# Pinning the early transfers of queries, keys, values and weight chunks to program order

## The chip, the cores and the metric

The kernel runs on one core of one Trainium2 chip. The metric is device time in microseconds (us), the median over several runs. An execution covers the whole chain: attention, a two-layer MLP, and a top-1 mixture of experts.

## The reference

Only what matters for the computation is kept:

```python
# attention: q, k, v are (4, 12, 448, 64)
scores = np.matmul(q, k.transpose(0, 1, 3, 2)) / np.sqrt(64)
scores = np.where(np.triu(np.ones((448, 448), bool), k=1), -1e9, scores)
attn = np.exp(scores - scores.max(-1, keepdims=True))
x = np.matmul(attn / (attn.sum(-1, keepdims=True) + 1e-9), v)   # -> (1792, 768)
# first MLP: w_in (768, 2048), w_out (2048, 768)
h = x @ w_in
x = (h - np.tanh(h)) @ w_out
# second: 8 experts, one for each token by argmax(x @ w_gate)
#   out = gate * sigmoid(x @ w_output_gate) * (relu(x @ w1[e]) @ w2[e])
```

All of it is float32. The kernel reaches that precision in the wide matmuls by splitting an operand into a high and a low part and adding three products.

## The kernel before

Attention works on 24 pairs of heads, six for each of four batch entries. For a pair, TensorE makes the scores of two heads (L351 for the first six pairs, in which the two heads sit in the two halves of the array's rows; L342 from the seventh pair on, with split operands), VectorE adds the mask and takes the row maxima (L371), ScalarE takes the exponential (L379), TensorE transposes the probabilities (L409), ScalarE or VectorE copy them out of PSUM (L417, L419, L423), and TensorE multiplies them with the values (L448). For the first six pairs the row sums are spread by small matmuls (`pd`, L432), VectorE multiplies the value with their reciprocals (L453, tile `ds`), ScalarE makes the high part (L461, `xh`) and VectorE the low part (L463, `xl`) of the result, which is the input of the first MLP.

The weights `w_in` come as sixteen raw chunks of 768 KB each (L142). A `Decoder` turns each into floats: one multiplication on ScalarE (L149), three operations on VectorE (L155, L156, L159), and then the split on ScalarE and VectorE (L84, L85). One or two are decoded for each pair, as the list `DECODE` says; each time the second step ends, the next chunk is fetched. `w_out` follows in the same way and goes back to memory.

The main loop runs over pairs and, within one, over a list of steps (`EARLY` for the first six, `ORDER` for the others): S scores, P transposes of the pair before, F the last score rows of the pair after, N the sums, A the value of the pair before. Loads of pair n + 2 are written at step N of pair n. From the first pair of the second batch on, matmuls of the first MLP (L480) are filled in between the steps; in the first batch only two groups of them run ahead, six matmuls a pair. Short dummy matmuls (L509, `warm`) stand between the steps of the first two pairs, pinned to program order.

All these instructions go through a scheduler that orders each engine's queue itself, by what it takes to be ready; each engine then works through its queue strictly in that order, and a waiting instruction holds up all behind it. `keep_in_program_order` pins an instruction behind the one that was written before it for the same engine. SyncE issues nearly all transfers, so its queue is the order of the transfers. Buffers matter too: `v` has two buffers, so the values of pair n + 2 wait for the value matmuls of pair n; `qh` and `kh` have two each, and from the seventh pair on `q` and `k` one each.

Of the kernel before, what the change touches and what calls it, by code (L numbers as in the profile page):

```python
# [19 lines left out]
P = 128  # L20
# [26 lines left out]
SCORES2 = 6  # L47

AHEAD = 2

LATER = (1, 1, 2, 2, 1, 0, 0, 0)

# [3 lines left out]
class Weights:  # L56


    def __init__(self, nc, pool, nslots):
        self.nc = nc  # L60
        self.slots = [(pool, n) for n in range(nslots)]
        self.pos = 0
# [60 lines left out]
class Decoder:  # L123
# [4 lines left out]
    def __init__(self, nc, stage):  # L128
        self.nc, self.stage = nc, stage
        self.jobs, self.ready, self.done, self.state = [], [], [], None  # L130


    keep = staticmethod(lambda x: x)

    def add(self, src, place, then):

# [2 lines left out]
    def fetch(self, n=1):  # L139
        for src, place, then in self.jobs[:n]:  # L140
            raw = place()
            self.nc.sync.dma_start(raw.rearrange("p a b -> p (a b)"), src)  # L142
            self.ready.append((raw, then))
        del self.jobs[:n]

# [7 lines left out]
    def second(self):  # L153
        vec, y, raw = self.nc.vector, self.y, self.raw
        self.keep(vec.tensor_scalar(y, y, 3, None, op0=ALU.logical_shift_left))  # L155
        vec.scalar_tensor_tensor(  # L156
            y, raw[:, :, 0], 29, y, op0=ALU.logical_shift_right, op1=ALU.bitwise_or
        )
        vec.scalar_tensor_tensor(  # L159
            y, raw[:, :, 1], -(1 << 31), y, op0=ALU.bitwise_and, op1=ALU.bitwise_or  # L160
        )
        self.done.append((y.bitcast(F32), self.ready.pop(0)[1]))
        self.fetch()

    def third(self):
        y, then = self.done.pop(0)
# [38 lines left out]
def attention_mlp1(tc, consts, ring, qk, v, w_in, w_out, wo, gT):  # L205


    nc = tc.nc
# [7 lines left out]
    NB = S // P  # L216
    TL = S - NB * P
# [10 lines left out]
    QC = 2 * S + TL  # L228
# [25 lines left out]
    stage = ctx.enter_context(tc.tile_pool(name="stage", bufs=1))  # L254
    dec = Decoder(nc, stage)
    win = []
    dec.keep = tc.keep_in_program_order
    free = [n for n in range(NF // 2, NF)] + [n for n in range(3 * NF // 4, NF)] + [NF - 2, NF - 1]

    def aside():  # L260
# [13 lines left out]
    def flush():  # L274
        while late:
            late.pop(0)()

    class Pair:
        def __init__(self, n):
            self.n, self.b, self.hp = n, n // NP, n % NP  # L280
            self.pr = prs[n % 2]
            self.two = n >= SCORES2

            self.divided = n >= NP

        def load(self):
            if self.two:
                self.q = ap.tile([P, QC], F32, tag="q", name="q", bufs=1)
                self.k = ap.tile([P, 2 * S], F32, tag="k", name="k", bufs=1)
            else:  # L290
                self.q = ap.tile([P, QC], F32R, tag="qh", name="q").bitcast(F32)
                self.k = ap.tile([P, 2 * S], F32R, tag="kh", name="k").bitcast(F32)
            for h in range(2):
                eng = nc.scalar if self.n == 0 and h else nc.sync
                s = slice(h * D, (h + 1) * D)

                c = slice(0, QC) if self.two else slice(h * (S + TL), h * (S + TL) + S)
                eng.dma_start(self.q[s, c], qk[self.n][:, c])
                c = slice(0, 2 * S) if self.two else slice(h * S, (h + 1) * S)
                eng.dma_start(self.k[s, c], qk[self.n][:, QC + c.start:QC + c.stop])  # L300

        def load_v(self):
            vt = ap.tile([P, NK, 2 * D], F32, tag="v", name="v")
            nc.sync.dma_start(
                vt[:, :NB], v[self.n, :NB * P].rearrange("(p c) d -> p c d", c=NB)
            )
            nc.sync.dma_start(vt[:TL, NB], v[self.n, NB * P:])
            self.v = vt.rearrange("p c (j d) -> p c j d", j=2)

        def split(self):  # L310
# [158 lines left out]
    def ahead(kd):  # L469

        for f in range(2):
            if kd == 0:
                begun.append(mps.tile([P, S], F32, tag="h", name="h"))
            for _ in mlp1_part(0, xT[0], f, begun[f], kd):
                pass
# [9 lines left out]
    def mlp1(b, xT, after=None):  # L485
        for f in range(NF):
            has = b == 0 and f < len(begun)
            ph = begun[f] if has else mps.tile([P, S], F32, tag="h", name="h")
            for kd in range(KD - 1 if has else 0, KD):
                for n in mlp1_part(b, xT, f, ph, kd):  # L490
                    if kd == KD - 1 and n == 2:
                        g = mp.tile([P, S], F32, tag="g", name="g", bufs=2)
                        nc.scalar.activation(g, ph, AF.Tanh)  # L493
                        nc.vector.tensor_tensor(g, ph, g, op=ALU.subtract)  # L494
                        nc.sync.dma_start(gT[f * P:(f + 1) * P, b * S:(b + 1) * S], g)
                        if after:
                            after(f)
                    yield
# [7 lines left out]
    def keep_busy(n):  # L506
        for _ in range(n):
            ph = mps.tile([P, S], F32, tag="h", name="warm")
            x = nc.tensor.matmul(  # L509
                ph.rearrange("p (a b) -> p a b", a=2), idle[:, :P],  # L510
                idle.unsqueeze(1).to_broadcast([P, 2, S // 2]), start=True, stop=True,
            )
            tc.keep_in_program_order(x)
# [10 lines left out]
    for i in range(len(pairs) + 1):  # L524
        cur = pairs[i] if i < len(pairs) else None
        nxt = pairs[i + 1] if i + 1 < len(pairs) else None
        prv = pairs[i - 1] if i > 0 else None
        todo = DECODE[i] if i < len(DECODE) else 0
        order = EARLY if i < NP else ORDER
        total = sum(FILL.get(o[0], 0) for o in order)  # L530
        begin = [n * len(order) // todo for n in range(todo)]
        acc, done = 0.0, 0
        for step, (op, *arg) in enumerate(order):
            if op == "F" and i + 1 < NP:
                nxt.score((rows[-1],))
            elif op == "S" and cur:
                cur.score(*arg)
            elif op == "N" and cur:
                cur.norm(*arg)
                if i + 2 < len(pairs):  # L540
                    pairs[i + 2].load()
                    pairs[i + 2].load_v()
                if i == 0:
                    dec.fetch(3)
            elif op == "P" and prv:
                prv.turn_p(*arg)
            elif op == "A" and prv:
                prv.value(xT[prv.b])
            elif op == "T" and nxt:
                nxt.split()  # L550
            if i < 2:
                keep_busy(WARM[i + 1])
            if 2 <= i <= NP and step == AHEAD:
                ahead(i - 2)
            acc += FILL.get(op, 0) * (per_b0 if i <= 2 * NP else per) / total
            fill.run(round(acc) - done)
            done = round(acc)
            flush()
            if i == 3:
                dec.keep = lambda x: x  # L560
            if dec.tick(bool(begin) and step >= begin[0]):
                begin.pop(0)
        if prv and prv.hp == NP - 1 and prv.b < B - 1:
            fill.add(mlp1(prv.b, xT[prv.b]))
# [649 lines left out]
def fused(ctx, tc, qk, v, w_in, w_out, gw, gates, w12, out):  # L1214
# [42 lines left out]

    consts["turnover"] = turnover
    last = attention_mlp1(tc, consts, ring, qk, v, w_in, w_out, wo, gT)

    xg, early, late, close = mlp2_route(
# [66 lines left out]
```

## Time and profile before

| what | value |
|---|---|
| median of 3 runs | 1017.88 us (1017.08 to 1018.27) |
| profiled execution, own time | 1015.92 us |
| its span, first to last instruction | 1014.2 us |
| TensorE matmuls busy | 989.7 us (98%) |
| TensorE weight loads busy | 894.6 us (88%) |
| VectorE busy | 651.1 us (64%) |
| ScalarE busy | 485.8 us (48%) |
| moved by DMA | 176.50 MB, mean 174 GB/s |

The shares are means over stages with different limits. Of the profile's page, the line of 40 slices shows where: the weight loads are at four to eight tenths in the first five slices and at eight or nine tenths nearly everywhere behind them, while VectorE is at seven to nine tenths in slices two to seven. A slice is 25 us. So the change, which touches the first 150 us or so, has to be read from that stretch alone.

### The profile page before, as it was taken

How to read it: one execution, taken by the hardware profiler on the slowest of the kernel's cores; microseconds unless marked ns; L12 is line 12 of the kernel's file. 1: busy time of each engine (PE TensorE's matmuls, PEld its weight loads, DVE VectorE, ACT ScalarE, POOL GpSimd, SP SyncE). 2: the span in 40 equal slices, each digit the busy share in tenths (PEclk: the TensorE clock that was granted, in tenths of full speed). 3: DMA queues.
4: the chain of work that ended last, by engine and by line, in shares of the span. 5: the costliest groups of instructions: out<-in, count | busy, mean ns of one | idle time of the engine just before them, and what ended most of it. 6: DMA issues, size and time to landing. Idle time of an engine off the chain costs nothing.

```text
span 1014.2 us, 16674 instructions
## 1 busy us (share of the span) xinstructions
PE 989.7 (98%) x6166; PEld 894.6 (88%) x6166; DVE 651.1 (64%) x1453; ACT 485.8 (48%) x1021; POOL 77.3 (8%) x84
## 2 busy tenths in 40 slices
PE   9999999999999999999999999999899999999995
PEld 4566788888888889999999999989899999999995
DVE  5779898877877635436776777375664754665430
ACT  5678888676766534312121212263643654555330
POOL 1000000000000000000111112102211011111000
PEclk9999999999999999999999999999999999999998
DMA  8844556767665228462434252497767765774400
GB/s 287 204 126 131 164 177 195 238 195 220 210 208 185 105 97 262 145 206 77 145 90 144 59 146 90 120 338 220 254 220 237 240 213 155 253 250 131 182 9 33
DMA packets 89100, 176.50 MB, mean 174 GB/s; under 512 B 8818, under 2 KB 52072, under 8 KB 89010
## 3 DMA queue, kind: packets, MB, share of 16 engines
q1 hardware_dynamic: 84258, 157.37, 49.4%
q0 software_dynamic: 4304, 16.97, 5.1%
q8 instruction: 50, 0.82, 0.3%
q10 hardware_dynamic: 448, 1.02, 0.3%
q14 instruction: 40, 0.33, 0.1%
HBM read 142.81 MB, written 34.08 MB: 174 GB/s over the span
## 4 chain that ended last, share of the span: by engine, by line
PE 83%; DMA 6%; DVE 5%; ACT 3%; issue 2%; SPq 0%; POOL 0%; POOLq 0%; ACTq 0%; DVEq 0%
PE x2p L688 22%; PE h L480 18%; PE h L1103 14%; PE py L1123 14%; PE x L448 4%; PE pt L409 3%; PE s L342 3%; DMA k<-in_qk_dram 2%; PE s L351 2%; DMA glo<-gT 2%; PE tr L1091 1%; DMA wraw<-in_w_dram 1%; DMA wo<-dy 1%; DVE w L85 1%; PE warm L509 1%
## 5 line engine op out<-in xcount | busy, mean ns | idle before, releaser
L480 PE MATMUL h<-xh,w 128*128 128x448 f32 x768 | 228.1, 375 | 1.3 <-ACT xh L461 0.7
L688 PE MATMUL x2p<-w,ghi 128*128 128x384 f32 x896 | 228.9, 336 | 0.0
L688 PEld LDWEIGHTS x2p<-w,ghi 128*128 128x128 f32 x896 | 160.9, 188 | 0.3 <-issue 0.2
L1103 PE MATMUL h<-xh,w 128*128 128x256 f32 x864 | 156.9, 284 | 4.2 <-DVE h L1110 2.6
L1123 PE MATMUL py<-w,h 128*128 128x384 f32 x864 | 155.2, 336 | 0.0
L688 PE MATMUL x2p<-w,glo 128*128 128x384 f32 x448 | 149.9, 335 | 0.0
L1123 PEld LDWEIGHTS py<-w,h 128*128 128x128 f32 x864 | 149.1, 188 | 0.0
L480 PEld LDWEIGHTS h<-xh,w 128*128 128x128 f32 x768 | 138.3, 189 | 11.8 <-ACT xh L461 1.8
L85 DVE TENSOR_TENSOR w<-wraw,w 128x768 fp32r<-128x768 f32 x144 | 131.8, 954 | 21.3 <-ACT w L84 21.3
L480 PE MATMUL h<-xl,w 128*128 128x448 f32 x384 | 142.9, 374 | 0.0
L1103 PEld LDWEIGHTS h<-xh,w 128*128 128x128 f32 x864 | 134.7, 191 | 5.2 <-DVE h L1110 2.8
L84 ACT CAST w<-wraw 128x768 fp32r<-128x768 f32 x144 | 114.0, 830 | 36.8 <-PE py L1123 28.5
L1103 PE MATMUL h<-xl,w 128*128 128x256 f32 x432 | 122.1, 283 | 0.0
L379 ACT ACTIVATE pr<-pr,mx 128x384 f32<-128x384 f32 (+3 forms) x168 | 88.3, 527 | 54.5 <-DVE mx L371 48.2
L711 DVE CUSTOM_DVE_ANT_0 junk<-x,row 128x768 bf16<-128x768 f32 x88 | 84.2, 957 | 32.9 <-ACT x L697 30.6
L688 PEld LDWEIGHTS x2p<-w,glo 128*128 128x128 f32 x448 | 84.1, 188 | 0.2 <-issue 0.2
L1103 PEld LDWEIGHTS h<-xl,w 128*128 128x128 f32 x432 | 82.6, 191 | 0.4 <-issue 0.4
L480 PEld LDWEIGHTS h<-xl,w 128*128 128x128 f32 x384 | 72.1, 188 | 5.3 <-DVE dy L155 0.3
L371 DVE CUSTOM_DVE_ANT_0 pr<-s,mask 128x384 f32<-128x384 f32 (+1 forms) x144 | 57.0, 419 | 13.8 <-PE s L342 10.4
L494 DVE TENSOR_TENSOR g<-h,g 128x448 f32<-128x448 f32 x64 | 39.8, 622 | 38.5 <-ACT g L493 38.1
L409 PE MATMUL pt<-ident,pr 128*128 128x128 f32 x384 | 61.0, 275 | 2.7 <-ACT pT L417 1.3
L409 PEld LDWEIGHTS pt<-ident,pr 128*128 128x128 f32 x384 | 46.7, 140 | 16.9 <-DVE pT L419 2.5
(178 smaller groups left out, 1159.0 us busy)
## 6 DMA issues: line engine op xcount, KB each, us to landing
wraw<-in_w_dram SPq DMA_DIRECT2D x144, 384.0 KB, 5.4
gT<-g SPq DMA_DIRECT2D x64, 224.0 KB, 1.9
glo<-gT SPq DMA_DIRECT2D x14, 1024.0 KB, 7.0
draw<-in_w_out_dram SPq DMA_DIRECT2D x16, 768.0 KB, 4.6
raw<-in_w_in_dram SPq DMA_DIRECT2D x14, 768.0 KB, 8.6
q<-in_qk_dram SPq DMA_DIRECT2D x36, 240.0 KB, 4.1
k<-in_qk_dram SPq DMA_DIRECT2D x36, 224.0 KB, 4.3
wo<-dy SPq DMA_DIRECT2D x16, 384.0 KB, 3.4
```

The source lines that it names most:

```text
L84: self.nc.scalar.copy(t[:, 0, :], raw)
L85: self.nc.vector.tensor_tensor(t[:, 1, :], raw, t[:, 0, :].bitcast(F32), op=ALU.subtract)
L371: nc.vector.tensor_tensor_reduce(out=self.probs(r), in0=s[:, o[n]:o[n] + w], in1=m, scale=-0.125, scalar=3.0e38, op0=ALU.add, op1=ALU.min, ...
L379: nc.scalar.activation(pc, pc, AF.Exp, bias=self.mx[:, x:x + 1], scale=-1.0, accum_out=self.sm[:, x:x + 1],)
L409: nc.tensor.transpose(pt[:, n * P:(n + 1) * P], self.pr[:, o:o + P], ident)
L448: nc.tensor.matmul(px[j * D:(j + 1) * D, kc * P:], self.v[:n, kc, j, :], self.pT[:n, j, pcol[kc]:pcol[kc] + S - kc * P], start=(kc == 0), ...
L480: nc.tensor.matmul(ph, w[:, kd, :], x, start=(kd == 0 and n == 0), stop=(kd == KD - 1 and n == 2))
L494: nc.vector.tensor_tensor(g, ph, g, op=ALU.subtract)
L688: nc.tensor.matmul(px, a[:, f, :], w[:, 0, h * hn:(h + 1) * hn], start=(n == 0), stop=(n == 3 * NF - 1),)
L711: nc.vector.tensor_tensor_reduce(out=junk, in0=x2, in1=row, scale=1.0, scalar=0.0, op0=ALU.mult, op1=ALU.add, accum_out=to,)
L1103: nc.tensor.matmul(ph, wp[:, kd, :], a[:, kd].rearrange("p a b -> p (a b)"), start=(n == 0), stop=(n == 3 * KD - 1),)
L1123: nc.tensor.matmul(py, hs[f][a][:, c], w[:, 0, o * hn:(o + 1) * hn], start=(n == 0), stop=(n == 3 * KF - 1),)
```

## The change

The transfers of the raw chunks (L142) and of the first ten pairs' queries, keys and values (L298, L300, L304, L307) are pinned to program order on SyncE. The chunks are pinned until the loop is at the ninth pair. The chunks fetched at the start are still two, but at the end of the first pair four are asked for instead of three, and until then a decoded chunk asks for no new one (`hold`).

```diff
--- before.py
+++ after.py
@@ -48,6 +48,8 @@
 
 AHEAD = 2
 
+ORDERED = 10
+
 LATER = (1, 1, 2, 2, 1, 0, 0, 0)
 
 WARM = (12, 3, 1)
@@ -128,9 +130,10 @@
     def __init__(self, nc, stage):
         self.nc, self.stage = nc, stage
         self.jobs, self.ready, self.done, self.state = [], [], [], None
-
-
-    keep = staticmethod(lambda x: x)
+        self.hold = True
+
+
+    keep = ask = staticmethod(lambda x: x)
 
     def add(self, src, place, then):
 
@@ -139,7 +142,7 @@
     def fetch(self, n=1):
         for src, place, then in self.jobs[:n]:
             raw = place()
-            self.nc.sync.dma_start(raw.rearrange("p a b -> p (a b)"), src)
+            self.ask(self.nc.sync.dma_start(raw.rearrange("p a b -> p (a b)"), src))
             self.ready.append((raw, then))
         del self.jobs[:n]
 
@@ -160,7 +163,8 @@
             y, raw[:, :, 1], -(1 << 31), y, op0=ALU.bitwise_and, op1=ALU.bitwise_or
         )
         self.done.append((y.bitcast(F32), self.ready.pop(0)[1]))
-        self.fetch()
+        if not self.hold:
+            self.fetch()
 
     def third(self):
         y, then = self.done.pop(0)
@@ -254,7 +258,7 @@
     stage = ctx.enter_context(tc.tile_pool(name="stage", bufs=1))
     dec = Decoder(nc, stage)
     win = []
-    dec.keep = tc.keep_in_program_order
+    dec.keep = dec.ask = tc.keep_in_program_order
     free = [n for n in range(NF // 2, NF)] + [n for n in range(3 * NF // 4, NF)] + [NF - 2, NF - 1]
 
     def aside():
@@ -280,6 +284,8 @@
             self.n, self.b, self.hp = n, n // NP, n % NP
             self.pr = prs[n % 2]
             self.two = n >= SCORES2
+
+            self.ask = tc.keep_in_program_order if n < ORDERED else lambda x: x
 
             self.divided = n >= NP
 
@@ -295,16 +301,16 @@
                 s = slice(h * D, (h + 1) * D)
 
                 c = slice(0, QC) if self.two else slice(h * (S + TL), h * (S + TL) + S)
-                eng.dma_start(self.q[s, c], qk[self.n][:, c])
+                self.ask(eng.dma_start(self.q[s, c], qk[self.n][:, c]))
                 c = slice(0, 2 * S) if self.two else slice(h * S, (h + 1) * S)
-                eng.dma_start(self.k[s, c], qk[self.n][:, QC + c.start:QC + c.stop])
+                self.ask(eng.dma_start(self.k[s, c], qk[self.n][:, QC + c.start:QC + c.stop]))
 
         def load_v(self):
             vt = ap.tile([P, NK, 2 * D], F32, tag="v", name="v")
-            nc.sync.dma_start(
+            self.ask(nc.sync.dma_start(
                 vt[:, :NB], v[self.n, :NB * P].rearrange("(p c) d -> p c d", c=NB)
-            )
-            nc.sync.dma_start(vt[:TL, NB], v[self.n, NB * P:])
+            ))
+            self.ask(nc.sync.dma_start(vt[:TL, NB], v[self.n, NB * P:]))
             self.v = vt.rearrange("p c (j d) -> p c j d", j=2)
 
         def split(self):
@@ -541,7 +547,8 @@
                     pairs[i + 2].load()
                     pairs[i + 2].load_v()
                 if i == 0:
-                    dec.fetch(3)
+                    dec.fetch(4)
+                    dec.hold = False
             elif op == "P" and prv:
                 prv.turn_p(*arg)
             elif op == "A" and prv:
@@ -556,6 +563,8 @@
             fill.run(round(acc) - done)
             done = round(acc)
             flush()
+            if i == ORDERED - 2:
+                dec.ask = lambda x: x
             if i == 3:
                 dec.keep = lambda x: x
             if dec.tick(bool(begin) and step >= begin[0]):
```

Tile names carry numbers below where rows would read alike; the line numbers of the changed kernel are six higher for most lines (L351 is L357, L371 is L377, L448 is L454, L453 is L459, L463 is L469) and three higher in the decoder.

On SyncE, before, behind the second pair's loads (`raw` are chunks; `q_275` and `k_276` belong to the third pair, `q_389` to the fourth):

```order
L142 DMA raw9_161<-in_w_in_dram 128x1536
L142 DMA raw10_201<-in_w_in_dram 128x1536
L142 DMA raw11_249<-in_w_in_dram 128x1536
L142 DMA raw12_284<-in_w_in_dram 128x1536
L298 DMA q_275<-in_qk_dram 64x448
L300 DMA k_276<-in_qk_dram 64x448
L298 DMA q_275<-in_qk_dram 64x448
L300 DMA k_276<-in_qk_dram 64x448
L142 DMA raw13_286<-in_w_in_dram 128x1536
L142 DMA raw14_288<-in_w_in_dram 128x1536
L142 DMA raw15_333<-in_w_in_dram 128x1536
L298 DMA q_389<-in_qk_dram 64x448
```

and in the changed kernel (`q_271`, `k_272` and `v_277` belong to the third pair, `q_387` to the fourth):

```order
L304 DMA q_271<-in_qk_dram 64x448
L306 DMA k_272<-in_qk_dram 64x448
L304 DMA q_271<-in_qk_dram 64x448
L306 DMA k_272<-in_qk_dram 64x448
L310 DMA v_277<-in_v_dram 128x384
L313 DMA v_277<-in_v_dram 64x128
L145 DMA raw10_280<-in_w_in_dram 128x1536
L145 DMA raw11_282<-in_w_in_dram 128x1536
L145 DMA raw12_284<-in_w_in_dram 128x1536
L145 DMA raw13_286<-in_w_in_dram 128x1536
L145 DMA raw14_331<-in_w_in_dram 128x1536
L304 DMA q_387<-in_qk_dram 64x448
```

The third pair's queries, keys and now also its values stand in front of five chunks, and the fourth pair's queries and keys behind these.

On TensorE, before, around the second pair's value (`x_524`; `s_497`, `s_538` and `s_539` are scores of the fourth pair):

```order
L351 MATMUL s_497<-k_390,q_389 64x448 x2
L448 MATMUL x_524<-pT_443,v_158 64x448
L409 MATMUL pt_491<-ident_64,pr1_111 128x128 x2
L448 MATMUL x_524<-pT_443,v_158 64x448
L351 MATMUL s_538<-k_390,q_389 128x384
L432 MATMUL pd_513<-ident_64,sm_261 64x128 x6
L432 MATMUL pd_513<-ident_64,sm_261 64x64 x2
L448 MATMUL x_524<-pT_443,v_158 64x320 x2
L448 MATMUL x_524<-pT_443,v_158 64x192 x2
L448 MATMUL x_524<-pT_443,v_158 64x64 x2
L351 MATMUL s_539<-k_390,q_389 128x384
L351 MATMUL s_538<-k_390,q_389 128x128
```

and in the changed kernel, around the third pair's value (`x_631`), where the fourth pair's first scores (`s_495`) now stand:

```order
L415 MATMUL pt_598<-ident_64,pr0_110 128x128 x2
L438 MATMUL pd_620<-ident_64,sm_377 64x128 x6
L438 MATMUL pd_620<-ident_64,sm_377 64x64 x2
L454 MATMUL x_631<-pT_552,v_277 64x448
L454 MATMUL x_631<-pT_552,v_277 64x320 x2
L454 MATMUL x_631<-pT_552,v_277 64x192 x2
L454 MATMUL x_631<-pT_552,v_277 64x64 x2
L357 MATMUL s_495<-k_388,q_387 64x448
L486 MATMUL h_459<-xh2_641,w0_207 128x448 x2
L486 MATMUL h_463<-xh2_641,w1_253 128x448
L486 MATMUL h_459<-xl2_642,w0_207 128x448
L357 MATMUL s_495<-k_388,q_387 64x448
```

The fourth pair's scores have moved from in front of the second pair's value to behind the third pair's.

On VectorE, before, up to and behind the third pair's multiply (`ds_631`; `s_586` and `s_587` are scores of the fourth pair, `s_606` of the fifth):

```order
L371 ISA pr1_111,mx_495<-s_586,mask_96 128x256
L371 ISA mx_495 128x1
L159 SCALAR_TENSOR_TENSOR dy_552<-raw12_284,dy_552 128x768
L371 ISA pr1_111,mx_495<-s_587,mask_96 128x256
L371 ISA mx_495 128x1
L423 COPY pT_554<-pt_600 128x2x128
L371 ISA pr0_110,mx_604<-s_606,tmask_97 128x448
L371 ISA mx_604 128x1
L85 TENSOR_TENSOR w4_578<-dy_552,w4_578 128x768
L387 TENSOR_SCALAR sm_496<-sm_496 128x7
L453 TENSOR_TENSOR ds_631<-x_633,ds_631 128x448
L388 RECIPROCAL sm_496<-sm_496 128x7
```

and in the changed kernel, around the same multiply (`ds_629`; `s_495` and `s_536` are scores of the fourth pair):

```order
L429 COPY pT_552<-pt_598 128x2x128
L162 SCALAR_TENSOR_TENSOR dy_439<-raw11_282,dy_439 128x768
L459 TENSOR_TENSOR ds_629<-x_631,ds_629 128x448
L87 TENSOR_TENSOR w3_467<-dy_439,w3_467 128x768
L469 TENSOR_TENSOR xl2_642<-ds_629,xh2_641 128x448
L158 TENSOR_SCALAR dy_550<-dy_550 128x768
L377 ISA pr1_111,mx_493<-s_495,tmask_97 128x448
L377 ISA mx_493 128x1
L159 SCALAR_TENSOR_TENSOR dy_550<-raw12_284,dy_550 128x768
L377 ISA pr1_111,mx_493<-s_536,mask_96 128x384
L377 ISA mx_493 128x1
L377 ISA pr1_111,mx_493<-s_536,mask_96 128x128
```

All of the fourth pair's maxima now stand behind the third pair's multiply, where before they and the fifth pair's first one stood ahead of it.

## Rows read from the trace of the kernel before

**Rows 1.** Stretches: length, busy PE, PEld, DVE, ACT, POOL (instructions), clock, DMA share, GB/s.

```profile
0.00:25.00 25.00, 22.48 (x107) 10.03 (x107) 13.12 (x41) 14.70 (x38) 2.91 (x14) 1.00 0.89 285
75.00:100.00 25.00, 22.57 (x138) 17.98 (x137) 24.72 (x59) 20.81 (x49) 0.00 (x0) 1.00 0.42 124
400.00:450.00 50.00, 50.00 (x262) 47.51 (x261) 17.31 (x30) 13.15 (x21) 1.16 (x6) 1.00 0.53 172
```

**Rows 2.** SyncE's timeline: start and duration in us, engine, line, operation, tiles, count.

```profile
7.49 2.11 SPq L142 DMA_DIRECT2D raw<-in_w_in_dram  x4
...
28.67 0.33 SPq L304 DMA_DIRECT2D v<-in_v_dram  x1
```

**Rows 3.** All weight-chunk issues of L142: us from issue to landing.

```profile
DMA to landing us min/median/max: 4.1/6.5/12.9
```

**Rows 4.** TensorE's timeline, 22 to 53 us; in brackets idle time and releaser.

```profile
22.72 0.96 PE L351 MATMUL s<-k,q 64*64 64x448 f32 x2
...
23.86 0.93 PE L351 MATMUL s<-k,q 64*64 64x448 f32 x2 [0.17 <-DMA k<-in_qk_dram]
...
26.54 2.10 PE L448 MATMUL x<-pT,v 128*64 128x448 f32 x16
...
28.86 1.14 PE L351 MATMUL s<-k,q 64*128 64x384 f32 x8
...
29.93 0.98 PE L409 MATMUL pt<-ident,pr 128*128 128x128 f32 x7
...
33.61 0.97 PE L351 MATMUL s<-k,q 64*64 64x448 f32 x4
...
34.51 0.97 PE L448 MATMUL x<-pT,v 128*64 128x448 f32 x2
...
36.67 0.91 PE L351 MATMUL s<-k,q 64*128 64x384 f32 x2
...
38.84 1.35 PE L448 MATMUL x<-pT,v 128*64 128x320 f32 x12
...
40.12 1.13 PE L351 MATMUL s<-k,q 64*128 64x384 f32 x6
...
42.09 0.70 PE L351 MATMUL s<-k,q 64*128 64x256 f32 x2
...
45.13 0.96 PE L351 MATMUL s<-k,q 64*64 64x448 f32 x2
...
50.43 2.09 PE L448 MATMUL x<-pT,v 128*64 128x448 f32 x14
```

**Rows 5.** Stretches between two VectorE multiplies and a split, columns as in Rows 1.

```profile
28.75:52.64 23.89, 23.79 (x143) 13.37 (x144) 16.78 (x48) 16.41 (x46) 0.00 (x0) 1.00 0.73 175
52.64:89.02 36.38, 34.42 (x221) 22.64 (x220) 31.88 (x81) 28.17 (x71) 0.00 (x0) 1.00 0.47 139
```

**Rows 6.** Groups on VectorE, 28 to 90 us: busy us, mean ns, idle before.

```profile
L85 DVE TENSOR_TENSOR w<-dy,w 128x768 fp32r<-128x768 f32 x7 | 6.7, 956 | 3.4 <-ACT w L84 3.4
...
L155 DVE TENSOR_SCALAR dy<-dy 128x768 int32<-128x768 int32 x6 | 3.3, 548 | 0.3 <-ACT dy L149 0.3
...
L156 DVE SCALAR_TENSOR_TENSOR dy<-raw,dy 128x768 int32<-128x768 int32 x6 | 5.7, 952 | 0.0
...
L453 DVE TENSOR_TENSOR ds<-x,ds 128x448 f32<-128x448 f32 x6 | 3.7, 623 | 5.2 <-PE x L448 5.2
...
L371 DVE CUSTOM_DVE_ANT_0 pr<-s,tmask 128x448 f32<-128x448 f32 x5 | 3.0, 601 | 0.4 <-PE s L351 0.4
...
L371 DVE CUSTOM_DVE_ANT_0 pr<-s,mask 128x384 f32<-128x384 f32 x10 | 5.5, 551 | 0.0
...
L371 DVE CUSTOM_DVE_ANT_0 pr<-s,mask 128x256 f32<-128x256 f32 x10 | 4.0, 419 | 0.5 <-PE s L351 0.5
...
L371 DVE CUSTOM_DVE_ANT_0 pr<-s,mask 128x128 f32<-128x128 f32 x10 | 2.9, 285 | 0.0
```

**Rows 7.** VectorE's timeline near 90 us.

```profile
89.54 1.00 DVE L392 TENSOR_SCALAR pr<-pr,sm 128x128 f32<-128x128 f32 x4
```

## The prediction

> **What bounds the kernel now.** I read the table of stretches first [rows 1], then SyncE's timeline [rows 2], then TensorE's and VectorE's around it. From 400 to 450 us TensorE is busy all the time and its weight loads fill 47.51 of 50 us: nothing but less TensorE work helps there, and the change touches nothing there. In the first 100 us it is otherwise: the weight loads fill 10.03 of 25 us at the start and 17.98 of 25 us from 75 to 100, TensorE idles 2.5 and 2.4 us in those two stretches, and from 75 to 100 VectorE is busy for 24.72 of 25 us [rows 1]. [...]
>
> Pairs of heads are counted from 0, so the third pair is pair 2. Pair n's scores, maxima (VectorE L371), exponentials, transposes and value (TensorE L448) overlap with pair n+1's scores, and one weight chunk a pair is decoded beside them on VectorE. From about 92 us the first batch's MLP matmuls fill TensorE's holes, so a delay before that goes to the end, and one behind it mostly doesn't.
>
> **SyncE's order.** Before, five chunks stand in front of pair 2's q and k, the last four issued together from 7.49 us on [rows 2]; its k lands so late that the two halves of its last scores run apart, 0.96 and 0.93 us, with a wait of 0.17 us for k between [rows 4]. Afterwards two chunks stand there. Side by side, four such instructions take 0.97 us (33.61 in rows 4); from 22.72 to 24.79 are 2.07 us, so this saves 1.1 us, and pair 0's value ends at 27.5 us instead of 28.64.
>
> The price stands behind it in the queue. Pair 2's v goes into the buffer that pair 0's v leaves: before, it is issued at 28.67 us, just after pair 0's value (26.54 + 2.10) [rows 2, 4]. Pinned, it stands in front of five chunks and pair 3's q and k, which need none of this. Before, the first five chunks were all issued by 9.6 us [rows 2]; now all but two start behind 27.5 us, and pair 3's q and k behind them. A chunk lands 4.1 to 12.9 us after its issue [rows 3]. So the third chunk comes at 32 us or later, and pair 3's k by about 27.5 + 3 + 12.9 = 43.4 us (the 3 us are some six issues at 0.5 us each, by the 2.11 us for four in rows 2).
>
> **TensorE's order follows.** Before, pair 3's last scores stand in front of pair 1's value and its other scores among it; now all of pair 3's scores stand behind pair 2's value. Before, 23.9 us pass from the end of pair 0's value (28.64) to that of pair 2's (50.43 + 2.09 = 52.52) [rows 4]. Out of this stretch go pair 3's scores, 0.97 + 0.91 + 1.13 + 0.70 + 0.70 us (the last form stands twice, the second time at 43.90), and pair 4's last ones, twice 0.96 us: 6.3 us. Added are 0.7 us, since pair 2's 256-column scores now run singly: one alone takes 0.70 us, and for the 448-column ones a pair took what one takes alone (0.97 and 0.96). So pair 2's value can't end before 27.5 + 23.9 - 6.3 + 0.7 = 45.8 us. It doesn't end so early, because TensorE has nothing of another pair to do between a transpose, its copy out and the value, and on ScalarE the first copy of pair 1's transposes now stands behind four exponentials. The upper bound is the time that it took with that other work in it, 52.5 - 1.1 = 51.4 us. I take 49.0: I count some 3 us in hops through ScalarE and VectorE (for two pairs a copy-out, then the multiply at 0.62 us [rows 6] and two splits of its kind). By then pair 3's k has landed, so no wait for it is charged.
>
> **VectorE pays.** What left that stretch comes later on VectorE, which had little air there. I counted its order from pair 2's multiply (L453, third one) to pair 5's split (L463, sixth one), behind which the last MLP matmul of that stage runs. Before, this is the stretch from 52.64 to 89.02 us: 31.88 us busy of 36.38, 4.5 us idle [rows 5]. Afterwards the same stretch of the order also holds two chunk decodes more (six instead of four), eight maxima (two of each width) and four multiplies of pair 6's probabilities. Two decodes are 2 x (0.548 + 2 x 0.952 + 0.956) = 6.8 us, L159 being the same operation as L156; the maxima 2 x (0.601 + 0.551 + 0.419 + 0.285) = 3.7 us [rows 6]; the multiplies 1.0 us [rows 7]. That makes 11.5 us; the durations of neighbours overlap a little, so I take 11. The stretch then needs 42.9 us of VectorE without idling, 47.4 with the idling of before; I take 3 us of idling, since it is fuller. Pair 5's split ends at 49.0 + 0.1 + 45.9 = 95.0 us against 89.0: 6.0 us later. The bounds: 45.9 + 42.9 = 88.8 (0.2 us earlier) and 51.5 + 47.4 = 98.9 (9.9 later).
>
> **What comes back.** At that point seven transposes more are done, 0.98 us [rows 4]. And behind it pair 7's value, which stands in pieces before (0.97 + 0.97 + 1.35 = 3.29 us for such a value, 34.51 and 38.84), stands together (2.10 us): 1.2 us. The other pieces put together lie in front of that point, where VectorE decides, and are not counted again.
>
> Sum: 6.0 - 1.0 - 1.2 = 3.8 us, bounds -2.4 and +7.7. The profiled execution took 1015.92 us (span 1014.2 and 1.7 around it), so it would take 1019.7 us; the median of the runs shown lies 1.96 us above it, which gives 1021.7 us.
>
> Costed at nothing: the later transfers pinned up to pair 9 and the six chunks in flight instead of five. TensorE's fill hides them from 92 us on; without that cover it is the third rival.
>
> **Rivals.**
> First, TensorE gains and the kernel gets faster. Its new order puts halves side by side: 384-column scores of two pairs (0.91 + 1.13 apart, 1.14 together: 1.8 us for two), one pair's last scores (0.96 + 0.96 against 0.97: 0.95), two values (2.4), against 0.7 lost on the 256-column scores: 4.45 us less TensorE time over the stage. If VectorE's extra work hides in its idle time, the end of the stage moves by this and the 1.1 us, as far as 1012.3 us; with half of it eaten by waits, 1015. It decides if pair 2's value ends near 46 us and VectorE then never idles. For it: VectorE idles 7.1 of 23.9 us before 52.6 us [rows 5]. Against: that time lies in front of the work that was pushed back.
> Second, it evens out: value at 47 us, 1 us of idling, so 91.0 us, 2.0 late, and 2.2 back: 1017.7 us.
> Third, transfers come late beyond the order: q and k of pairs 6 to 8 have one buffer each and now stand behind up to two chunks and a v that waits. A landing at 12.9 instead of the median 6.5 us [rows 3] puts 6.4 us on top: 1028 us. Against: at 0.42 DMA share [rows 1] the queue is half empty there.
> Fourth, TensorE's clock falls. The granted clock is 1.00 in all rows, with 2.43 us of idling spread over 75 to 100 us [rows 1]. [...]
>
> **How the numbers follow.** Forecast (2 to 8 us slower) 0.58; first rival 0.17; second 0.17; third 0.05; fourth 0.03. A difference under 0.2% (2.0 us) can't be told from none. Faster takes the first rival, same the second with the forecast's lower edge: faster 0.17, same 0.19, slower 0.64. The forecast's own range is 1019 to 1026 us. For 8 in 10 the range goes down to 1015, at the bound of -2.4 us and half of the first rival, and up to 1027, past the bound of +7.7 us (1025.6).
>
> **What would show it.** Right: SyncE's v of pair 2 issued at about 27.5 us with five L145 issues behind it; a hole in the DMA rate before that; pair 3's first scores on TensorE at 47 us or later (33.61 before); VectorE over 95% busy between 60 and 95 us; the sixth L469 at about 95 us. Wrong: that split before 91 us, or TensorE waiting on DMA by more than 2 us in the first 100 us.

## The result: slower by 1.1%, outside the forecast's range

The changed kernel takes 1031.03 us (median of 4 runs, 1027.40 to 1033.80) against 1018.08 us before (1017.08 to 1022.36): ratio 1.0114, 95% interval 1.0087 to 1.0140, which is 9 to 14 us. The direction was right (64% on slower); the size was not: 1021.7 us was forecast, with 1027.0 us as the upper end. The profiled execution took 1033.8 us (span 1031.9) and is the slowest of the four, so its rows show rather more than the median does. One execution of a later version (after_spread) took 4581.28 us and is left out of that version's ratio.

### The profile after

The stretches of the changed kernel, columns as in [rows 1]:

```profile
0.00:25.00 25.00, 22.65 (x117) 10.64 (x118) 13.86 (x44) 13.92 (x37) 2.91 (x14) 1.00 0.43 137
25.00:50.00 25.00, 23.88 (x157) 14.32 (x155) 15.16 (x34) 14.07 (x33) 0.00 (x0) 1.00 0.78 254
50.00:75.00 25.00, 21.90 (x132) 12.31 (x130) 20.87 (x66) 19.97 (x58) 0.00 (x0) 0.93 0.45 121
75.00:100.00 25.00, 18.77 (x117) 14.79 (x115) 21.02 (x47) 17.12 (x37) 0.00 (x0) 0.86 0.46 129
100.00:150.00 50.00, 47.99 (x280) 39.76 (x279) 47.02 (x110) 40.68 (x96) 0.00 (x0) 1.00 0.64 188
150.00:200.00 50.00, 47.72 (x275) 39.97 (x275) 40.09 (x100) 34.79 (x82) 0.00 (x0) 0.97 0.71 210
250.00:300.00 50.00, 46.53 (x260) 39.12 (x260) 36.03 (x88) 32.00 (x73) 0.00 (x0) 0.93 0.60 178
```

and of the kernel before, those that [rows 1] don't hold:

```profile
25.00:50.00 25.00, 24.90 (x157) 13.97 (x155) 18.57 (x52) 16.41 (x45) 0.00 (x0) 1.00 0.81 200
50.00:75.00 25.00, 24.97 (x163) 15.32 (x161) 19.07 (x53) 19.43 (x49) 0.00 (x0) 1.00 0.44 136
100.00:150.00 50.00, 50.00 (x291) 39.73 (x292) 46.49 (x116) 39.97 (x92) 0.00 (x0) 1.00 0.57 169
150.00:200.00 50.00, 50.00 (x299) 42.72 (x300) 43.72 (x111) 38.01 (x88) 0.00 (x0) 1.00 0.70 210
250.00:300.00 50.00, 50.00 (x297) 42.53 (x296) 38.92 (x101) 35.04 (x87) 0.00 (x0) 1.00 0.69 212
```

Read the second number of each row (TensorE's busy time) and the clock near the end. From 25 to 100 us TensorE idles 1.1, 3.1 and 6.2 us, where it idled 0.1, 0.03 and 2.4 us before; another 2.0, 2.3 and 3.5 us go from 100 to 150, 150 to 200 and 250 to 300 us, where it never idled. In four of these stretches the granted clock is under 1.00 (0.93, 0.86, 0.97 and 0.93): it fell for a while, to 0.50 from 60 to 62 us and from 255.77 to 261 us. VectorE, which I had named as the bound, is less busy from 75 to 100 us than before (21.02 against 24.72 us). And the DMA share in the first 25 us is halved, 0.43 against 0.89: transfers that could run don't.

Why is in SyncE's timeline (start, duration, line, tiles, count):

```profile
27.75 0.33 SPq L310 DMA_DIRECT2D v<-in_v_dram  x1
...
28.64 3.29 SPq L145 DMA_DIRECT2D raw<-in_w_in_dram  x5
...
55.85 0.59 SPq L306 DMA_DIRECT2D k<-in_qk_dram  x1
66.74 0.33 SPq L310 DMA_DIRECT2D v<-in_v_dram  x1
...
67.69 0.53 SPq L145 DMA_DIRECT2D raw<-in_w_in_dram  x1
68.26 0.47 SPq L304 DMA_DIRECT2D q<-in_qk_dram  x1
```

The first two rows are the forecast to a quarter of a microsecond: pair 2's v is issued at 27.75 us (forecast 27.5), where pair 0's value ends, with five chunks behind it. The next ones are the part that I had costed at nothing. Pair 5's v waits for pair 3's value until 66.74 us, the queue stands from 56.4 to 66.7 us, and behind it stand one chunk and then the q and k of pair 6. These q and k are the first in their buffers, so no buffer holds them back. Before, they went out long ahead of that. They can be told by their size: each half of q is 240 KB from pair 6 on, and 112 KB up to pair 5. The first two such transfers on SyncE, and the cast that reads them, in the kernel before:

```profile
23.92 0.59 SPq L298 DMA_DIRECT2D q<-in_qk_dram  x1
...
31.41 0.60 SPq L298 DMA_DIRECT2D q<-in_qk_dram  x1
```

```profile
57.09 1.00 ACT L318 CAST qh<-q 128x960 fp32r<-128x960 f32 x1
```

So all of pair 6's q was under way 25 us before its cast, and now its halves go out 44 and 38 us later. That slack hid the first part of the delay and not the rest. In the changed kernel, the table of waits of SyncE from 50 to 100 us (who waits, for whom, us in total, times, the longest) names the value matmuls:

```profile
SPq L310 <- PE x L454: 23.9, 3, 10.2
```

On ScalarE the cast of this q then waits for the transfer:

```profile
77.30 0.99 ACT L324 CAST qh<-q 128x960 fp32r<-128x960 f32 x1 [2.54 <-DMA q<-in_qk_dram]
```

TensorE's timeline, what answers to [rows 4], and then its longest waits (in brackets the idle time and what ended it):

```profile
22.89 0.97 PE L357 MATMUL s<-k,q 64*64 64x448 f32 x4
...
25.61 2.10 PE L454 MATMUL x<-pT,v 128*64 128x448 f32 x16
...
44.13 2.09 PE L454 MATMUL x<-pT,v 128*64 128x448 f32 x14
46.05 0.91 PE L357 MATMUL s<-k,q 64*64 64x448 f32 x2
...
60.05 1.54 PE L415 MATMUL pt<-ident,pr 128*128 128x128 f32 x6 [1.23 <-DVE pT L425]
61.52 1.76 PE L357 MATMUL s<-k,q 64*64 64x448 f32 x4
...
80.19 0.89 PE L348 MATMUL s<-kh,qh 128*128 128x448 f32 x2 [2.94 <-ACT kh L326]
...
93.97 1.25 PE L348 MATMUL s<-kh,qh 128*128 128x448 f32 x3 [2.98 <-DVE qh L329]
...
168.31 0.55 PE L415 MATMUL pt<-ident,pr 128*128 128x128 f32 x3 [2.04 <-ACT pT L423]
...
255.77 0.69 PE L415 MATMUL pt<-ident,pr 128*128 128x128 f32 x2 [3.47 <-DVE pT L425]
```

Pair 2's last scores stand together (0.97 us) and pair 0's value ends at 27.7 us, as forecast; pair 3's first scores come at 46.05 instead of 33.61 us (47 or later forecast). The row at 61.52 shows the clock: four such scores take 1.76 us there, at a granted clock of 0.50 (61.50 to 63.30 us), and 0.97 us in the first row, in a stretch at 1.00. Behind the waits of 2.94 and 2.98 us the clock is 0.55 from 80.19 to 84 us and 0.52 from 93.97 to 97 us. The last two waits are of another kind. The copy that TensorE waits for stands on ScalarE and VectorE behind the decoder, and that waits for its one buffer of raw chunks or its one of decoded ones:

```profile
165.85 0.89 ACT L152 ACTIVATE dy<-draw 128x768 f32<-128x768 f32 x1 [1.67 <-DMA draw<-in_w_out_dram]
...
253.24 0.89 ACT L152 ACTIVATE dy<-draw 128x768 f32<-128x768 f32 x1 [4.05 <-DMA wo<-dy]
```

VectorE between the same multiplies and split as in [rows 5], and that split (the sixth L469):

```profile
27.83:46.27 18.44, 17.96 (x122) 11.74 (x122) 12.40 (x29) 11.42 (x28) 0.00 (x0) 1.00 0.93 312
46.27:97.92 51.65, 41.67 (x239) 26.27 (x238) 43.41 (x111) 37.17 (x94) 0.00 (x0) 0.90 0.48 132
```

```profile
97.32 0.62 DVE L469 TENSOR_TENSOR xl<-ds,xh 128x448 fp32r<-128x448 f32 x1
```

The first stretch lasts 18.4 us instead of 23.9, the second 51.7 instead of 36.4, with 43.41 us of VectorE's work (42.9 counted) and 8.2 us of idling (3 taken).

### The profile page after: what moved, and what is told of

Its sections match the earlier page's. It is cut to its first block, busy times and chain, and to the rows that moved or that the text cites. A ratio compares the mean times of both kernels' runs of the same rounds, so it can differ in the third digit from the quotient of the medians.

```text
span 1031.9 us, 16684 instructions
## 1 busy us (share of the span) xinstructions
PE 993.3 (96%) x6166; PEld 900.6 (87%) x6166; DVE 656.0 (64%) x1453; ACT 487.1 (47%) x1021; POOL 79.1 (8%) x84
## 4 chain that ended last, share of the span: by engine, by line
PE 81%; DMA 6%; DVE 5%; ACT 3%; issue 2%; SPq 0%; POOL 0%; POOLq 0%; ACTq 0%; DVEq 0%
PE x2p L697 22%; PE h L486 18%; PE h L1112 14%; PE py L1132 14%; PE x L454 4%; PE s L348 3%; PE pt L415 3%; DMA glo<-gT 2%; DMA wo<-dy 1%; PE warm L515 1%; PE tr L1100 1%; PE s L357 1%; ACT pr L385 1%; DMA wraw<-in_w_dram 1%; DMA q<-in_qk_dram 1%
## 5 line engine op out<-in xcount | busy, mean ns | idle before, releaser
L486 PE MATMUL h<-xh,w 128*128 128x448 f32 x768 | 230.5, 378 | 2.4 <-DVE g L500 1.3
L415 PE MATMUL pt<-ident,pr 128*128 128x128 f32 x384 | 63.7, 282 | 10.2 <-DVE pT L425 5.4
L377 DVE CUSTOM_DVE_ANT_0 pr<-s,mask 128x384 f32<-128x384 f32 (+1 forms) x144 | 55.9, 420 | 19.3 <-PE s L348 15.0
```

Source lines behind the costliest of these rows:

```text
L377: nc.vector.tensor_tensor_reduce(out=self.probs(r), in0=s[:, o[n]:o[n] + w], in1=m, scale=-0.125, scalar=3.0e38, op0=ALU.add, op1=ALU.min, ...
L415: nc.tensor.transpose(pt[:, n * P:(n + 1) * P], self.pr[:, o:o + P], ident)
L486: nc.tensor.matmul(ph, w[:, kd, :], x, start=(kd == 0 and n == 0), stop=(kd == KD - 1 and n == 2))
```

## The experiments

Theory A: pair 2's v holds the queue early (the forecast), and pair 5's v does the same to the q and k of pair 6 (the third rival), and both together make the loss. Theory B: only the second matters. Theory C: the clock is what costs. Theory D: pins of the chunks, or two chunks in front, are the loss. All ratios are against the kernel before, run on the same chip, with their 95% intervals; the changed kernel itself was timed only in the runs above. Pieces of an edit that are left out are marked with " ...".

**Early waits away.** Pair 2's v gets a place of its own; the order of transfers stays the same.

```diff
+            if self.n == 2:
+                vt = ap.tile([P, 2 * S], F32, tag="k", name="v", bufs=1)
+                vt = vt[:, :2 * D * NK].rearrange("p (c d) -> p c d", c=NK)
+            else:
                 vt = ap.tile([P, NK, 2 * D], F32, tag="v", name="v")
```

> SyncE's order is that of the changed kernel, transfer for transfer, but the third pair's v lies in a place of its own, so that the v of pairs 2, 3 and 4 waits for no value. Theory (the early waits of v hold the queue: about 4 us of my sum and some of the rest): chunk three is issued by 16 us, pair 3's q and k by 20 us, and the time is 1018 to 1022 us. Rival (the loss comes from pair 5's v, which holds pair 6's q and k, two waits of 3 us at 80 and 94 us, and the clock behind them): these waits stay, and the time is 1026 to 1031 us.

1.0062 (1.0038 to 1.0087), 1025.61 us: between the two. The chunks go out at 16.54 us. The waits of v are not all gone before that of pair 5: the v of pairs 3 and 4 still hold SyncE for 8.5 us in the first 50 us, which I had not expected. The pinned v of pair 5 still holds pair 6's q, and TensorE's wait stays; SyncE's and then TensorE's rows:

```profile
16.54 2.85 SPq L145 DMA_DIRECT2D raw<-in_w_in_dram  x5
...
63.90 0.33 SPq L314 DMA_DIRECT2D v<-in_v_dram  x1
...
65.42 0.47 SPq L304 DMA_DIRECT2D q<-in_qk_dram  x1
```

```profile
76.67 0.82 PE L352 MATMUL s<-kh,qh 128*128 128x448 f32 x3 [2.19 <-ACT kh L330]
...
89.34 1.02 PE L352 MATMUL s<-kh,qh 128*128 128x448 f32 x3 [2.98 <-DVE qh L333]
```

**The complement.** Only pair 2's v is pinned; that of later pairs is free, and the rest is pinned past it.

```diff
+            self.ask_v = self.ask if n < 3 or n >= ORDERED else free_v
 ...
-            self.ask(nc.sync.dma_start(
+            self.ask_v(nc.sync.dma_start(
 ...
```

> The complement: pair 2's v stays pinned in front of the five chunks, the v of pairs 3 to 9 is free, and chunks, q and k are pinned to one another past it. Theory (early waits): five chunks still at 28 us, pair 3's scores on TensorE behind pair 2's value, 1022 to 1027 us. Rival (pair 5's v): pair 6's q and k come before it, no wait of 3 us for the casts of pair 6, 1016 to 1021 us.

1.0054 (1.0033 to 1.0075), 1025.26 us, in the range of the early theory. Pair 2's v goes out at 27.65 us, the sixth split comes at 94.75 us (95.0 forecast), and the cost is 5.5 us (3.8 forecast). But this is not the forecast's mechanism by itself. Only one half of pair 6's q goes out before pair 5's v; the scheduler put the unpinned v next, where it waits from 61.7 to 66.6 us, and the other half and both halves of k stand behind it:

```profile
61.20 0.47 SPq L324 DMA_DIRECT2D q<-in_qk_dram  x1
66.58 0.33 SPq L330 DMA_DIRECT2D v<-in_v_dram  x1
...
67.47 0.59 SPq L326 DMA_DIRECT2D k<-in_qk_dram  x1
68.11 0.59 SPq L324 DMA_DIRECT2D q<-in_qk_dram  x1
68.75 0.59 SPq L326 DMA_DIRECT2D k<-in_qk_dram  x1
```

The later wait is thus shorter, not gone. Pair 6's cast comes at 72.71 instead of 77.30 us and waits for no transfer, and in place of TensorE's waits of 2.94 and 2.98 us stands one of 2.15 us, at 90.24 us, for ScalarE's probabilities:

```profile
72.71 0.98 ACT L344 CAST qh<-q 128x960 fp32r<-128x960 f32 x1
```

```profile
90.24 0.97 PE L435 MATMUL pt<-ident,pr 128*128 128x128 f32 x4 [2.15 <-ACT pr L418]
```

**Both away.** Every v is written behind the value that frees its buffer, so that little stands behind one that waits. All other pins, and the two chunks in front, stay.

```diff
                     pairs[i + 2].load()
-                    pairs[i + 2].load_v()
 ...
                 prv.value(xT[prv.b])
+                if nxt:
+                    nxt.load_v()
```

> Every v is issued behind the value that frees its buffer, in program order, so that no transfer stands behind a v that waits; all else as changed. If both waits of v make up the loss: 1016 to 1019 us, at or under the kernel before, no row of stretches before 100 us with a clock under 1.00. If the loss is in the pins of chunks or in two chunks in front of pair 2: over 1023 us.

> v_late once more on this chip, for the comparison with v_late_spread, and since it is the one that beats the kernel before: 0.995 to 0.999 if that was no chance.

0.9971 (0.9952 to 0.9989), 1016.81 us, and in a second session 0.9982 (0.9968 to 0.9995): faster than before by 0.2 to 0.3%, twice. So theory D falls, since the pins of the chunks and the two chunks in front are all still there, and A stands: the place of the v in the queue costs the whole loss and hides a small gain of the rest. SyncE now waits 5.6 us for values from 50 to 112 us, where it waited 25.6 us in the changed kernel, and pair 6's q goes out at 58.4 us. Its pinned chunks wait 21.8 us there, and that costs nothing that shows. Against this version the early waits cost at most 0.0054 + 0.0029 = 0.8% (8.5 us) and the later ones at most 0.0062 + 0.0029 = 0.9% (9.3 us): each of the two runs keeps some of the waits that the other was to measure, and together they cost 1.0114 - 0.9971 = 1.4%, less than the sum of 1.7%. That each is about half stays an estimate. Three further edits of this version, below, leave the place of the v alone, and each made it slower by some 0.5%, so no split finer than that can be read from these runs. My marker for the clock was wrong here, since one wait of 2.67 us is left at 88 us with 0.93 in its stretch:

```profile
75.00:100.00 25.00, 21.14 (x130) 16.40 (x127) 24.07 (x58) 20.86 (x51) 0.00 (x0) 0.93 0.38 99
```

**Four chunks in front**, as v_late otherwise (no hold, three chunks behind).

```diff
-        if not self.hold:
-            self.fetch()
+        self.fetch()
 ...
-                    dec.fetch(4)
+                    dec.fetch(3)
```

> As v_late, but with four chunks in front of pair 2's q and k instead of two (no hold, three chunks behind). By my first step this costs 1.0 us or less against v_late, since pair 2's last scores wait for k again; if the two chunks in front are themselves a loss (chunks come late to the decoder), this is 2 us or more faster than v_late.

1.0189 (1.0165 to 1.0213), 1038.57 us: neither. What it shows is the same trap with another transfer. A pinned chunk, whose buffer VectorE still reads for the decoder, holds SyncE from 76 to 98 us; pair 7's q and k stand behind it, and TensorE waits 13.37 us for that pair's scores. SyncE's rows (the duration of the first spans two issues with the wait between), its waits from 70 to 112 us, and TensorE's row:

```profile
75.69 22.99 SPq L145 DMA_DIRECT2D raw<-in_w_in_dram  x2
98.78 0.47 SPq L303 DMA_DIRECT2D q<-in_qk_dram  x1
```

```profile
SPq L145 <- DVE dy L162: 31.3, 3, 22.3
```

```profile
110.33 1.03 PE L347 MATMUL s<-kh,qh 128*128 128x448 f32 x2 [13.37 <-ACT ds L444]
```

So it doesn't measure what two chunks in front are worth; that wasn't settled.

**The clock.** Matmuls of no use fill TensorE's waits in the changed kernel (8 behind pair 4's value, 12 behind pair 5's) and in v_late (12 behind pair 5's).

```diff
+WARM2 = {5: 8, 6: 12}
 ...
                 prv.value(xT[prv.b])
+                if i in WARM2:
+                    ph = ps.tile([P, 512], F32, tag="s", name="warm", bufs=3)[:, :S]
+                    for _ in range(WARM2[i]):
+                        tc.keep_in_program_order(nc.tensor.matmul(...))
```

> The changed kernel with 8 matmuls of no use behind pair 4's value and 12 behind pair 5's, which fill the two waits of 2.94 and 2.98 us for pair 6's and 7's casts; their results are read by nothing. Theory (the granted clock falls in these waits, and the half speed behind them, 0.86 on the mean from 75 to 100 us, costs some 3 us): the clock stays at 1.00 from 76 to 100 us and the time falls by 2 to 4 us, to a ratio of 1.007 to 1.010 against before. Rival (VectorE and the transfers set these 25 us, half speed is hidden behind them): the same ratio as the changed kernel, 1.0114, or more by what the matmuls put in the way.

> v_late with 12 matmuls of no use behind pair 5's value, in its wait of 2.67 us at 85.4 us; their results are read by nothing. If the clock behind that wait costs, 1 to 2 us under v_late: a ratio of 0.995 to 0.996 against before. If it doesn't: 0.997, as v_late.

In the changed kernel the clock stays at 1.00 from 75 to 100 us:

```profile
75.00:100.00 25.00, 23.41 (x155) 16.65 (x152) 23.33 (x51) 19.65 (x45) 0.00 (x0) 1.00 0.52 141
```

but the ratio is 1.0099 (1.0078 to 1.0120): 1.5 us less than 1.0114, with intervals that overlap, so not told from nothing. In v_late the clock stays at 1.00 as well, and the time goes up, to 1.0021 (1.0008 to 1.0034). Theory C falls as the main cause: with the clock held from 75 to 100 us a loss of 0.8 to 1.2% is left, and in v_late holding it bought less than the matmuls and the new order behind them cost. What the falls near 60, 169 and 255 us cost wasn't tested. In v2_only_dec, below, the clock is 1.00 from 25 to 400 us, against three falls in v2_only, and the ratios are 1.0058 and 1.0054.

**VectorE.** One decode is moved out of the stretch that I said VectorE bounds; the chunks stay pinned for one round more.

```diff
-DECODE = [2, 1, 1, 1, 1, 2, 1, 2, 1, 2, 1, 1] + [2, 1, 1] * 4
+DECODE = [2, 1, 1, 1, 1, 1, 1, 2, 2, 2, 1, 1] + [2, 1, 1] * 4
 ...
-            if i == ORDERED - 2:
+            if i == ORDERED - 1:
```

> v2_only with one chunk's decode (0.55 + 2 x 0.95 + 0.96 = 3.4 us of VectorE) moved from the sixth round of the loop to the ninth, behind the stretch that I said VectorE bounds. Theory (VectorE sets the end of that stretch): the sixth split comes 3 us earlier than 94.8 us, and the ratio falls from 1.0054 to 1.002 to 1.003. Rival (waits of TensorE on copies and its half clock set it, VectorE has 6.7 us of idle time there): the split moves by under 1 us and the ratio stays at 1.005.

> v_late with the same decode moved as in v2_only_dec. If VectorE bounds 75 to 100 us (24.07 of 25 us busy in v_late): 2 to 3 us under v_late, ratio 0.994 to 0.995. If not, or if the moved decode is late for the MLP: 0.997 or more.

The sixth split comes 4.75 us earlier; the row of v2_only, then that of v2_only_dec:

```profile
94.75 0.62 DVE L489 TENSOR_TENSOR xl<-ds,xh 128x448 fp32r<-128x448 f32 x1
```

```profile
90.00 0.62 DVE L489 TENSOR_TENSOR xl<-ds,xh 128x448 fp32r<-128x448 f32 x1
```

and yet the time doesn't move: 1.0058 (1.0034 to 1.0081) against 1.0054, and for v_late 1.0018 (0.9999 to 1.0038), slower than without. So an earlier split alone doesn't bring an earlier end, which my prediction had taken for granted. In v2_only_dec TensorE idles 1.7, 1.6 and 2.5 us from 200 to 250, 250 to 300 and 300 to 350 us (v2_only: 0.8, 0.5 and 0): what was won is given back there. Whether the later decode does that, or the order that the scheduler made of it, stays open.

**The late waits.** From the thirteenth round on the decodes of the second matrix are spread evenly.

```diff
+        if i >= 12:
+            begin = [[0, 10], [7], [4]][i % 3][:todo]
```

> The changed kernel with the decodes of the second weight matrix (from the 13th round of the loop on) spread evenly: of four decodes in three rounds the starts stand at steps 0 and 10, 7, 4 of 13 instead of 0 and 6, 0, 0. Each of them needs the one buffer for raw chunks loaded again and the one for decoded chunks stored. Theory (the waits of TensorE of 2.04 us at 168 us and 3.47 us at 255 us come from this chain, which is held too tight): the first wait is ahead of the edit and stays, the second one goes or falls under 1 us, and the time falls by 3 to 5 us, to a ratio of 1.007 to 1.009. Rival (it is chance, the chain waits on single slow transfers wherever it stands): 1.0114, with a wait of 1 us or more between 200 and 370 us.

> v_late with the same spread. Theory: its wait of 1.34 us at 242 us goes, 1 to 2 us under v_late, a ratio of 0.995 to 0.996 against before. Rival: 0.997, as v_late.

1.0122 (1.0099 to 1.0145), with a wait of 2.61 us at 234 us: the rival stands. For v_late it is 1.0031 (1.0015 to 1.0047), slower than the 0.9982 of the same session, which neither side had expected; the even spread costs some 0.5% there, and why stays open. The 3.47 us at 255 us in the changed kernel stand behind a wait of 4.05 us of ScalarE's decode for one transfer. From 60 to 420 us that decode waits 10.6 us in all, six times, for such transfers there (`wo<-dy`), and 15.1 us, eleven times, in after_spread. The two profiles of v_late differ too: in the first TensorE waits 1.34 us at 242 us, in the second it idles nowhere from 200 to 350 us. So they come and go between executions; whether the changed kernel has more of them than the kernel before, one profile of each can't say.

## Why the prediction was wrong

- **Step one (SyncE, two chunks in front): right.** Pair 2's scores together, pair 0's value 0.9 us earlier (1.1 forecast).
- **Step two (pair 2's v holds the queue): right**, 27.75 us, and no wait for pair 3's k followed.
- **Step three (pair 2's value at 49.0 us): too late.** It ends at 46.2 us, near the lower bound of 45.8: hardly any of the 3 us of hops shows.
- **Step four (VectorE pays): the work right, the idling wrong.** 43.4 us of work (42.9 counted), but 8.2 us of idling instead of 3, so the split comes at 97.3 us and not at 95.0. VectorE over 95% busy was my marker; it was busy for 28.40 of the 35 us from 60 to 95, 81%. It waited itself: of the idling in these 35 us, 2.9 us were for ScalarE's first step of the decode, and 1.0 and 1.4 us for pair 6's cast and scores, which waited for q. With most of the later waits gone (v2_only) the kernel lost 5.5 us where the sum had 3.8, and 3.8 is inside the interval of 3.4 to 7.6.
- **The step that failed: "Costed at nothing: the later transfers pinned up to pair 9 ... TensorE's fill hides them from 92 us on."** The wait of pair 5's v begins at 56 us, before that fill, and delays pair 6's q and k, which TensorE could have used at 77 us. Without most of the early waits, these pins cost 6.3 us (v2_own). My third rival named the queue and "a v that waits", at a chance of 0.05, but priced a slow landing, and "against" it I put that the queue is half empty by DMA share. The share speaks of the transfers, not of the queue: SyncE stood still for 10 us, with a DMA share of 0.23 from 56.4 to 66.7 us, because the instruction at its head waited. I had written down that rule for pair 2's v and not applied it to pair 5's.
- **The fourth rival (the clock)** came true in the rows: five falls, three of them before 100 us. By the rows all five together can have cost 10 us at most (1.00 less the clock, times the length); the two that were held off in the experiment gave back 1.5 us, which can't be told from nothing. Behind waits of 1.99 to 3.63 us the clock mostly fell, but not each time (below).
- **The sum by TensorE's idle time** might have served better than one engine's finish; this is an account after the fact. Up to 400 us TensorE idles 14 us more than before by the stretches of both profiles, the lower clock takes 10 us at most, and the halves put side by side would give back the 4.45 us of the first rival, as estimated there: 20 us at most, against 17.7 us between the two spans.

## What to carry to other kernels

When transfers are pinned in one queue, go through every pinned one that waits for a buffer, not the first alone: write down when that buffer comes free, what stands behind it that could go earlier, and when that is needed. Pin a transfer behind the work that frees its buffer, and the order can stay: that turned 1.1% of loss into 0.2 to 0.3% of gain here. Don't build on so small a gain: three small changes of that kernel's order each took it back. Where one engine is full for the rest of a stage, count its idle time and not when another engine finishes.

## What the runs showed of the hardware

The granted clock fell behind some waits of TensorE and not behind others of the same length. After a wait of 1.23 us for transposes near 60 us it was 0.58 from 60 to 64 us in the changed kernel, but 1.00 from 60.4 to 64 us in v2_only_dec after a wait of the same length at the same place. Behind waits of 1.99 to 3.63 us it mostly fell, to 0.50 to 0.79 over the 3 to 5 us that follow: 0.63 behind 1.99 us at 130.5 us in v2_only, 0.79 behind 2.39 us at 94.8 us and 0.69 behind 3.63 us at 81.8 us in after_spread, 0.50 behind 3.47 us at 255.77 us in the changed kernel. Yet it stayed at 1.00 behind 2.19 us at 76.67 us in v2_own, behind 2.08 us at 77.71 us in v_late_4ahead and behind 2.61 us at 234.45 us in after_spread:

```profile
234.45:238.00 3.55, 3.55 (x23) 3.28 (x24) 2.44 (x9) 2.38 (x8) 0.00 (x0) 1.00 0.81 283
```

In the changed kernel the rows were at full speed again within 6 us of the wait's end (longest behind the wait that ends at 255.77 us: 0.50 to 261 us, 1.00 from 261.8 us on), so that a fall cost 3 us at most by my estimate, 6 us at 0.50. In v_late_4ahead, where more waits followed, it stayed low for longer: 0.50 from 89.5 to 98 us and still 0.50 from 110 to 113 us, behind the wait of 13.37 us.
